# Loading q, k and v of a batch pair one step sooner in an attention + spectral-mix kernel

## The chip, the cores and the metric

The kernel runs on one core of a Trainium2 chip. The metric is device time in microseconds for one execution; lower is better. Seven runs of the kernel before the change are at hand, and one further execution that the hardware profiler recorded.

## The reference, cut to what matters

Batch 8, 8 heads, sequence 576, head width 64, so a model width of 512. All inputs and the output are float32.

```python
# attention with a forget gate
scores = q @ k.T / sqrt(64);  cum = cumsum(log(clip(f, 1e-4, 1)))
scores = where(causal, -1e9, scores + cum[:, None] - cum[None, :])
x = softmax(scores) @ v                     # -> (8, 576, 512)
# spectral mix
X = rfft(x, axis=1)[:, :64]                 # 64 modes
Yr = Xr @ w_r[m] - Xi @ w_i[m];  Yi = Xr @ w_i[m] + Xi @ w_r[m]   # per mode, 512 x 512
u = x + irfft(Y, n=576);  out = u + relu(u @ w_ch)
```

The weights w_r and w_i are 64 matrices of 512 x 512 each; they make up most of what is read from memory.

## The kernel before, in words

**Two stages.** In the first, attention runs as 32 steps (`NS`), numbered s. A step handles one head for two batches. Two steps with the same s // 2 form a *pair*, `pr`: it covers two batches and two heads, and there are 16 of them (`NPR`). They run over four channel blocks dc (two heads each), and in each block over four batch pairs bp. The loop over s stands at L649. In the second stage (from L683), the rest of the spectral mix, the product with w_ch and the output are made.

**What a pair needs.** `emit_loads(pr)` (L215) issues three DMAs, for k, q and v, from the Pool engine's queue into one of three staging sets (`STG` = 3, chosen by pr % 3). Only the first v goes by the SP queue. `emit_transposes(pr, what)` (L429) then copies the staged k, q or v on VectorE into a bf16 tile (kb, qb at L437; vb at L441), transposes it on TensorE (L455, tile tp), and copies the result out of PSUM: k and v on ScalarE (L468, L472), q on VectorE (L470). k and q of pair pr + 1 are handled at the even step of pair pr, v at its odd step (L658). A staging set is free for the next load once kb, qb and vb of its pair have been read from it.

**What a step does.** `emit_scores` (L499) makes scores in four pieces on TensorE (L507) and the exponential on ScalarE (L514). `emit_av` (L531) multiplies the exponentials of the step before by v (L552, tile pav) and divides by their sum on VectorE (L563, L574). `emit_vback` (L474) turns v back into rows (L479, then the copies L485 and L486). After the last step of a pair, `emit_dft` (L576) makes the 64 modes of the finished channels (L595; a first version for dc < 2 also has L620).

**The weights.** There are 64 weight tiles (`NT`), each of two DMAs of 512 KB, issued by `emit_w_load` (L91) on the Pool queue into a ring of nine buffers (`NRING`), named wb. `emit_modes(n)` (L118) consumes tile n: 32 small matmuls (L146) into the tile A, of which there is one PSUM buffer during attention, then one VectorE copy or addition out of it (L155, L157, or L161 for tiles 32 to 63). Only after that can the next tile's matmuls begin. From step 9 on, tiles 0 to 31 are consumed during attention, and each is followed by the load of the tile nine further on (L666 to L670). Tiles 32 to 63 need the spectrum of the last channel block and come after attention.

**What sets the order.** Every DMA of `pool_dma` (L88), and so every load of q, k, v and of weights after the first v, stays on the Pool queue in the order in which the program emits it. In steps 0 to 8 the loop mixes both kinds: `emit_loads(pr + 2)` at even steps (L651), weight tiles 2 to 8 by the rule of L653, and w_ch at step 9 (L655). The order of the instructions on TensorE, VectorE and ScalarE is not that of the source: a scheduler lays it down when the program is built, by when it reckons the operands of an instruction to be there. The copies kb, qb, vb of the first three pairs are the exception (L450).

## Time and profile before

| | us |
|---|---|
| median of 7 runs | 452.76 |
| lowest, highest | 450.14, 455.41 |
| the seven runs | 455.41, 450.17, 454.04, 450.58, 450.14, 453.12, 452.76 |
| the profiled execution, its own time | 454.45 |
| its span, first to last instruction | 452.6 |

The profile puts these shares of the span on the engines: PE (TensorE matmuls) 344.6 us or 76%, VectorE 239.9 us or 53%, ScalarE 197.6 us or 44%, Pool 138.9 us or 31%. The mean clock granted to TensorE was 0.774 of full speed. The core moved 97.27 MB by DMA, at 215 GB/s over the span.

In the profile, L146 is line 146 of the program; PE, PEld, DVE, ACT, POOL are TensorE's matmuls, its weight loads, VectorE, ScalarE and GpSimd. A timeline row gives the start in us, the duration, the engine, the line, the operation with output<-input, the number of instructions that were merged, and in square brackets the idle time ahead of it and what ended that idle time. A row of the window view gives a stretch of time, the busy us of each engine in it (with the number of instructions), the granted TensorE clock, the DMA share and GB/s. The three strips with 40 entries cut the span into slices of 11.3 us.

The pairs can be followed by the start of the copy kb, the first thing done with a pair's data:

| pair | 3 | 4 | 5 | 6 | 7 | 8 | 9 | 10 | 11 | 12 | 13 | 14 | 15 |
|---|---|---|---|---|---|---|---|---|---|---|---|---|---|
| kb starts, us | 45.53 | 58.74 | 70.34 | 87.66 | 107.67 | 127.11 | 147.28 | 165.75 | 184.14 | 201.76 | 218.71 | 236.53 | 255.91 |

### The profile page before, as it was taken

The numbers are of one execution on the slowest core, as the hardware profiler recorded it, in microseconds if no ns is written. First come the engines' busy times: TensorE is split into PE (matmuls) and PEld (weight loads), VectorE is DVE, ScalarE is ACT, GpSimd is POOL, SyncE is SP. The second block draws the span as 40 slices with busy tenths as digits, with TensorE's granted clock in tenths as the row PEclk, the third lists the DMA queues.
The fourth block names the chain that finished last, engine by engine and source line by source line (L and its number), as shares of the span: only waits on it lengthen the run. The fifth ranks groups of instructions, "written<-read, shape, count | busy, mean of one in ns | idle before, by whom it ended". The sixth has DMA issues, their size and how long they took to land.

```text
span 452.6 us, 11206 instructions
## 1 busy us (share of the span) xinstructions
PE 344.6 (76%) x4823; PEld 237.1 (52%) x4823; DVE 239.9 (53%) x614; ACT 197.6 (44%) x296; POOL 138.9 (31%) x195
## 2 busy tenths in 40 slices
PE   2786788987888879879778796999994247427992
PEld 1453656776666656656566574656673124323440
DVE  6677778675564655546547577333321002103993
ACT  3787478763536364364364554343330002102442
POOL 8233330532332232332332310123343232200660
PEclk9998799996756665566566778799995559856998
DMA  9999999899999999999999999699999999991697
GB/s 193 223 236 237 235 238 235 141 237 226 221 235 229 218 236 231 216 235 211 237 237 211 211 212 209 115 164 186 211 211 211 211 211 211 212 210 27 222 379 265
DMA packets 49920, 97.27 MB, mean 215 GB/s; under 512 B 3376, under 2 KB 12080, under 8 KB 49872
## 3 DMA queue, kind: packets, MB, share of 16 engines
q0 software_dynamic: 46240, 85.93, 97.4%
q1 hardware_dynamic: 3552, 10.50, 6.5%
q8 instruction: 38, 0.62, 0.5%
q10 hardware_dynamic: 80, 0.13, 0.1%
q14 instruction: 10, 0.08, 0.0%
HBM read 163.73 MB, written 9.44 MB: 383 GB/s over the span
## 4 chain that ended last, share of the span: by engine, by line
PE 46%; DMA 16%; ACT 12%; DVE 10%; issue 4%; POOL 0%; DVEq 0%; ACTq 0%
DMA wb<-in_moe_w_i_dram 16%; ACT E L514 8%; PE A L146 7%; PE pav L552 7%; PE pxw L731 7%; PE ps L507 7%; PE tp L455 5%; PE px L595 2%; DVE QTs L470 2%; PE vp L479 2%; PE ptr L720 2%; ACT KT L468 2%; ACT VT L472 2%; PE pz L834 1%; DVE E L529 1%
## 5 line engine op out<-in xcount | busy, mean ns | idle before, releaser
L514 ACT ACTIVATE E<-ps 128x1024 bf16<-128x1024 f32 (+1 forms) x128 | 101.1, 853 | 26.3 <-PE ps L507 17.7
L146 PE MATMUL A<-XT,wb 128*128 128x16 bf16 x2048 | 70.9, 182 | 45.1 <-DMA wb<-in_moe_w_i_dram 24.1
L146 PEld LDWEIGHTS <-wb 128*128 128x128 bf16 x2048 | 63.7, 101 | 56.7 <-DMA wb<-in_moe_w_i_dram 26.0
L89 POOL DMA_DIRECT2D wb<-in_moe_w_r_dram x65 | 43.2, 665 | 154.0 <-PE A L146 39.1
L507 PE MATMUL ps<-QTs,KT 64*128 64x64 bf16 (+4 forms) x384 | 59.0, 334 | 17.1 <-ACT E L514 15.7
L89 POOL DMA_DIRECT2D wb<-in_moe_w_i_dram x65 | 43.2, 665 | 65.1 <-DMA wb<-in_moe_w_r_dram 32.4
L552 PE MATMUL pav<-va,E 128*128 128x65 bf16 (+1 forms) x1088 | 57.1, 214 | 5.7 <-DVE x_all L574 4.0
L552 PEld LDWEIGHTS <-E 128*128 128x128 bf16 (+1 forms) x1088 | 47.4, 118 | 19.0 <-issue 8.1
L529 DVE TENSOR_TENSOR E<-E,trimask 128x256 bf16<-128x256 bf16 (+2 forms) x128 | 37.0, 301 | 22.4 <-ACT E L514 22.3
L161 DVE TENSOR_TENSOR YT<-A,Yacc 128x128 bf16<-128x128 f32 x24 | 8.9, 370 | 64.8 <-PE A L146 64.8
L472 ACT COPY VT<-tp 128x640 bf16<-128x640 bf16 (+1 forms) x32 | 23.3, 758 | 35.2 <-PE tp L455 35.1
L507 PEld LDWEIGHTS <-KT 64*128 64x128 bf16 x384 | 19.6, 101 | 33.0 <-issue 24.6
L731 PE MATMUL pxw<-wch,yy 128*128 128x512 bf16 x144 | 33.7, 384 | 0.0
L738 ACT CAST XW<-pxw 128x512 bf16<-128x512 f32 x36 | 20.3, 587 | 30.0 <-PE pxw L731 30.0
L468 ACT COPY KT<-tp 128x640 bf16<-128x640 bf16 (+1 forms) x32 | 22.0, 752 | 25.3 <-PE tp L455 25.3
L470 DVE COPY QTs<-tp 128x640 bf16<-128x640 bf16 (+1 forms) x32 | 23.2, 767 | 16.3 <-PE tp L455 16.3
L574 DVE TENSOR_TENSOR x_all<-pav,rcp 128x384 bf16<-128x384 f32 x64 | 29.0, 454 | 0.8
L563 DVE RECIPROCAL rcp<-pav 128x6 f32<-128x6 f32 x64 | 12.1, 190 | 27.6 <-PE pav L552 26.8
L879 POOL TENSOR_TENSOR uo<-uo 128x1024 f32<-128x1024 f32 x7 | 16.5, 2358 | 30.4 <-DVE uo L872 26.7
L750 ACT CAST yy<-pyw 128x512 bf16<-128x512 f32 x8 | 4.7, 586 | 48.2 <-PE pyw L743 48.2
L441 DVE TENSOR_TENSOR vb<-stv,wdec 128x1152 bf16<-128x1152 f32 x16 | 21.6, 1348 | 2.0 <-PE tp L455 2.0
L731 PEld LDWEIGHTS <-yy 128*128 128x128 bf16 x144 | 13.5, 99 | 16.8 <-DVE yy L725 4.5
(115 smaller groups left out, 467.9 us busy)
## 6 DMA issues: line engine op xcount, KB each, us to landing
wb<-in_moe_w_r_dram POOLq DMA_DIRECT2D x63, 512.0 KB, 16.2
wb<-in_moe_w_i_dram POOLq DMA_DIRECT2D x63, 512.0 KB, 16.5
stv<-in_v_dram POOLq DMA_DIRECT2D x15, 576.0 KB, 15.1
out_dram<-uo SPq DMA_DIRECT2D x16, 512.0 KB, 3.7
stk<-in_k_dram POOLq DMA_DIRECT2D x16, 288.0 KB, 15.4
stq<-in_q_dram POOLq DMA_DIRECT2D x16, 288.0 KB, 15.2
out_dram<-uo SPq DMA_DIRECT2D x7, 128.0 KB, 4.4
stv<-in_v_dram SPq DMA_DIRECT2D x1, 576.0 KB, 4.1
```

Of the source, the lines that this page charges most:

```text
L89: tc.keep_in_program_order(nc.gpsimd.dma_start(dst, src))
L146: nc.tensor.matmul(A[:, eb, mi, :], lhsT=w_of(mi, eb * 128), rhs=x_of(m), start=(i == 0), stop=(i == len(terms) - 1),)
L455: nc.tensor.transpose(tp[:, r - r0, :, :].rearrange("c h p -> c (h p)"), sb[:, r, :, :].rearrange("p b d -> p (b d)"), ident_bf[:, :],)
L468: nc.scalar.copy(rows(KTs[pr % 2][:, :, 0:S]), tv)
L470: nc.vector.tensor_copy(rows(QT[pr][:, :, :]), tv)
L472: nc.scalar.copy(rows(VTs[pr % 2][:, :, 0:S]), tv)
L507: nc.tensor.matmul(ps[:, b, o : o + n], lhsT=KTs[pr % 2][bs, h, jb * 128 : (jb + 1) * 128], rhs=QT[pr][bs, h, jb * 128 + c0 : jb * 128 + c ...
L514: nc.scalar.activation(E[:, :, piece * 512 : piece * 512 + w], ps[:, :, 0:w], ACT.Exp, scale=scale,)
L529: nc.vector.tensor_tensor(dg, dg, tr, ALU.mult)
L552: nc.tensor.matmul(pav[64 * half : 64 * half + w, slot, :], lhsT=E[:, b, c : c + (w - 1) * st + 1 : st], rhs=va[:, jb, b, :], start=(n == ...
L574: nc.vector.tensor_tensor(xo, pi, ri, ALU.mult)
L731: nc.tensor.matmul(pxw[:, :], lhsT=xT[:, eb, i * 128 : (i + 1) * 128], rhs=wch[:, eb, :], start=(eb == 0), stop=(eb == NDC - 1),)
```

## The change: the pair's loads move ahead of one weight tile

The call of `emit_loads` moves from the even step of a pair to the odd step before it. The pair that is loaded, the staging set and all shapes stay as they are.

```diff
         for s in range(NS + 1):
             pr, h = s // 2, s % 2
-            if h == 0 and pr + STG - 1 < NPR:
-                emit_loads(pr + STG - 1)
+            if s == 0:
+                emit_loads(STG - 1)
+            if h == 1 and pr + STG < NPR:
+                emit_loads(pr + STG)
             if s < 10 and nload < min(NRING, 3 + 3 * s // 4):
                 next_w()
             if s == 9:
```

At step s = 2 pr + 1 the program now loads pair pr + 3 into the set of pair pr, whose last copy (vb) is emitted at step 2 pr - 1. Before, the same load stood at step 2 pr + 2. The weight tiles and w_ch that lay between the two places on the Pool queue now come after the three DMAs.

## The prediction

> **What bounds the kernel.** I read the strips first, then Pool's timeline, then windows by pair, then PE's timeline. The strips (TensorE clock, DMA share, GB/s; slices of 11.3 us) suggest a kernel bound by its transfers:

> ```profile
> PEclk9998799996756665566566778799995559856998
> DMA  9999999899999999999999999699999999991697
> GB/s 193 223 236 237 235 238 235 141 237 226 221 235 229 218 236 231 216 235 211 237 237 211 211 212 209 115 164 186 211 211 211 211 211 211 212 210 27 222 379 265
> ```

> But the rate has two holes: 141 GB/s in the eighth slice, and 115 to 186 in the three slices from 283 us. Pool's timeline (start, duration, operation, idle time before it) has both:

> ```profile
> 66.23 0.74 POOL L89 DMA_DIRECT2D wch<-in_moe_w_ch_dram  x1 [1.85 <-DMA wb<-in_moe_w_i_dram]
> 83.16 0.62 POOL L89 DMA_DIRECT2D wb<-in_moe_w_r_dram  x1 [16.19 <-PE ps L507]
> ...
> 270.80 0.72 POOL L89 DMA_DIRECT2D wb<-in_moe_w_r_dram  x1 [8.75 <-PE A L146]
> 271.51 0.72 POOL L89 DMA_DIRECT2D wb<-in_moe_w_i_dram  x1
> 286.68 0.71 POOL L89 DMA_DIRECT2D wb<-in_moe_w_r_dram  x1 [14.45 <-PE A L146]
> ```

> At 66 us Pool has filled the ring of nine and stands until tile 0 is consumed (81.8 to 82.9 us). At 262 and 272 it stands again: the ring is full, the transfers are ahead of the arithmetic. The issue at 286.68 is tile 41, which needs the buffer of tile 32, and tile 32 needs the spectrum of the last pair. So **attention's arithmetic sets the time up to 286 us**, and what follows (166 us: 23 tiles at some 5.0 us each from 286.7, a thin start until 306, and about 42 us of output) hangs on that moment. The chain of waits agrees: its 16% of "DMA wb" all stand after 338 us.

> Is attention waiting for q, k, v? Pair 7's loads are issued at 84.4 to 85.8 us; such loads land about 15 us later (the issue table's median), so by 101; kb of pair 7 starts at 107.67. Pair 3: issued from 18.5, landed by 39, used at 45.53. Pair 5: 42.7 to 47.8, landed by 63, used at 70.34. No pair waits for its data. What is late is the *place* of the copy in VectorE's queue. PE's timeline and the windows before pair 7:

> ```profile
> 104.54 1.12 PE L146 MATMUL A<-XT,wb 128*128 128x16 bf16 x32 [0.52 <-DVE Yacc L155]
> 106.17 1.12 PE L146 MATMUL A<-XT,wb 128*128 128x16 bf16 x32 [0.52 <-DVE Yacc L155]
> 107.80 1.16 PE L146 MATMUL A<-XT,wb 128*128 128x16 bf16 x32 [0.52 <-DVE Yacc L155]
> ...
> 109.53 0.75 ACT L468 COPY KT<-tp 128x640 bf16<-128x640 bf16 x1 [5.56 <-PE tp L455]
> ```

> Weight tiles in a row, 1.63 us apart, each waiting 0.52 us for the single A buffer, ScalarE idle for 5.56 us, and pair 7 behind them. Windows (busy us of PE, PEld, DVE, ACT, POOL; clock; DMA; GB/s):

> ```profile
> 58.70:70.30 11.60, 9.87 (x142) 6.59 (x140) 10.07 (x30) 9.15 (x15) 3.42 (x5) 1.00 1.12 221
> 87.70:107.70 20.00, 16.95 (x366) 13.77 (x366) 13.21 (x41) 11.89 (x18) 6.54 (x11) 0.93 1.13 225
> 107.70:127.10 19.40, 16.16 (x239) 12.23 (x239) 11.29 (x32) 9.11 (x14) 6.04 (x10) 0.68 1.14 231
> ...
> 106.00:108.00 2.00, 1.32 (x39) 1.23 (x39) 0.79 (x3) 0.00 (x0) 0.62 (x1) 0.50 1.12 210
> ```

> Full clock until the row of tiles, then half clock for some 14 us; that pattern repeats for every later pair.

> **The change, part by part.** No instruction is added or dropped: the same 15 x 3 Pool loads. Two things move.

> *Pool's queue.* Pairs 3 and 5 keep their place (no weight tile lies between). Pairs 4, 6 and 8 to 15 pass one tile (two DMAs), pair 7 passes tile 9 and w_ch. Do the earlier loads wait for their staging set? Pair 7 would go at about 66 us; its set is last read by vb of pair 4, 61.6 to 62.9. Pair 6: about 52 us against 50.2. Pair 10: about 123 against 114.4. No new wait, though pair 6 has only some 2 us. Queued behind a late one would be weight tiles, which are used 25 us or more after issue here. w_ch slips by about 5 us to 71 and is used at 288. Cost: 0. The gain of pair 7 lying in the hole at 80 to 88 us is that of more bytes moved, which is lost again at 262 to 287, where the ring is full: 0.

> *The engines' order.* In the built program of the change, copies and transposes of a pair stand earlier among PE's work for pairs 4 to 7. Weight tiles consumed between one pair's k transposes and the next:

> ```
> pair to pair  5-6  6-7   7-8   8-9 9-10 10-11 11-12 12-13 13-14 14-15 15-end
> before         3    7     3     2   3    3     2     3     3     2     1
> after          1    4.7   5.3   3   3    2     3     3     2     3     2
> row of A matmuls that ends it:  before 116 (at 6-7); after 52 (at 7-8)
> ```

> So the first long row comes one pair later and is 64 matmuls shorter. (a) Two tiles fewer stand in that row: 2 x 1.63 = -3.3 us. (b) They return: one joins the row that ends 14-15, +1.6; the other (tile 31) now stands between the last vp and pav, where PE is idle 1.18 us anyway for the copy va (277.39 us, waiting on L485): 1.1 us of matmuls, 0. (c) Pair 7 now runs before the first row, at full clock. The same instructions at full and half clock, pair 6 against pair 7 (us): tk 0.68/1.12, tq 0.83/1.19, vp 0.44/0.69, px 0.89/1.40, scores 0.99/1.63, pav 0.78/1.23 and 0.69/1.02, px2 0.61/1.04, tv 0.44/0.74. Sum 6.35 against 10.06: -3.7 us, nearly all of it on the chain of waits, which between 108 and 118 us consists of PE. From below it is 0, if the clock drops within the pair all the same.

> [...] I take -2.3 for (c), nearer to the row; not all of it, because seven runs of one program spread over 5.3 us, so the slow stretches can't fall alike in each.

> Sum: -3.3 + 1.6 + 0 - 2.3 = **-4.0 us**. The tail keeps its 166 us: tile 40 is now issued some 9 us ahead of tile 32's end instead of 16, and needs about 7 (the quickest DMA of wb took 5.0 us to land, and there are two at some 2.2 us each). The profiled execution is 454.45, so 450.4; it lies 1.7 above the median. From the median of 452.76: **448.8 us**.

> **Rivals.**
> [...]
> 2. *The kernel is transfer-bound after all*, and the hole is what is gained: 4 us at 68 and 4 at 159 GB/s against 235 lack 2.8 + 1.3 = 4.1 us, giving 448.7 with the end of the weights 4.1 earlier. For it: DMA at 9 in nearly all slices. Against: the two ring waits at 262 and 272. Hence unlikely as a cause.
> 3. *Slower: the clock drops one pair earlier.* In pairs 4 and 5 all nine k transposes, then 16 pav matmuls, now stand ahead of the step's second score piece. If ScalarE runs dry there, PE waits for exponentials, thins out between 75 and 95 us, and pair 6 goes at half clock as well as pair 7: +3.7, with (a) and (b) -1.7, and up to 1.5 for the delayed pieces: 452.76 + 3.5 = 456.3. [...] Against: ScalarE copies KT until 62.0 before it takes that piece, so a delay of 1.2 us is mostly hidden.
> 4. *Nothing happens*, because no load was late: 452.8. The changed order of the engines speaks against it.

> **Numbers.** Half a per cent, 2.3 us, is what a measurement of this kernel can tell from no change. Forecast 0.46, rival 1 0.20, rival 2 0.04, rival 3 0.20, rival 4 0.10. The forecast's own range is 446.5 (all of (c), and 0.9 of run-to-run shift) to 450.5. The range takes in rivals 1, 2 and 4 and part of 3: 446 to 456. Faster by over 0.5% (under 450.5): forecast, rival 2 and a little of rival 1 = 0.52. Within: most of 1, rival 4, a little of 3 = 0.27. Slower: 0.21.

> **What would show it.** Right: the eighth slice's GB/s near 235, while kb of pair 8 starts 5 to 8 us sooner (119 to 122 us) and the clock stays at 1.00 until about 112; ScalarE's 5.56 us wait is gone or halved; tile 41 is issued near 283. [...] Rival 3: a low clock between 85 and 100. Wrong altogether: kb or vb waiting for stk, stq or stv, or Pool idle for a VectorE read ahead of one of these loads.

## The result and the profile after

The changed kernel takes 445.25 us (median of 12 runs, 443.68 to 449.87); the kernel before took 452.34 us in the 31 runs beside them. The ratio is **0.9872, with a 95% interval of 0.9842 to 0.9902**: of 452.34 that is 5.8 us less (4.4 to 7.1), where the prediction had 4.0 less. Some executions of a kernel fall in a slower state with a lower granted clock (of the 27 of the kernel before beside e1 to e4 it is 6, with a mean clock of 0.749 to 0.778, against 0.793 for the other 21); all ratios here leave them out, the medians do not, and so a quotient of two medians differs a little from the ratio. The profiled execution of the changed kernel took 446.41 us, its span is 444.0 us, and the mean granted clock 0.790. Its strips, in slices of 11.1 us:

```profile
PEclk9997699996557666668578698899995559756999
DMA  9999999999999999999999999899999999991697
GB/s 189 229 235 255 219 237 238 235 232 217 237 210 237 236 211 237 212 236 237 211 237 211 211 211 211 153 186 198 211 211 211 211 211 211 212 210 29 224 378 279
```

Of the two holes in the rate, the first is closed (eighth slice 235 in place of 141) and the second is still there (153 to 198). Pool's timeline shows both. The row at 70.87 is w_ch, which has slipped behind the loads of pair 7; the next ring wait ends at 82.37; the last row is tile 41.

```profile
70.87 0.76 POOL L89 DMA_DIRECT2D wch<-in_moe_w_ch_dram  x1 [0.40 <-DMA stv<-in_v_dram]
82.37 0.61 POOL L89 DMA_DIRECT2D wb<-in_moe_w_r_dram  x1 [10.74 <-PE vp L479]
...
263.61 0.72 POOL L89 DMA_DIRECT2D wb<-in_moe_w_r_dram  x1 [9.76 <-PE A L146]
270.19 0.71 POOL L89 DMA_DIRECT2D wb<-in_moe_w_r_dram  x1 [5.14 <-PE A L146]
279.06 0.71 POOL L89 DMA_DIRECT2D wb<-in_moe_w_r_dram  x1 [7.44 <-PE A L146]
```

Tile 41 is issued at 279.06, 7.6 us sooner than before (286.68), and the end of the span comes 8.6 sooner, 452.6 to 444.0. So nearly the whole gain is there when attention ends: from the end of tile 32 to the end of the span it is 166.2 us before and 165.2 after.

A single pair of profiles overstates the gain: 454.45 - 446.41 = 8.0 us, against 5.8 by the ratio. Over 21 executions of the kernel before, those that count in the ratios of e1 to e4 below, each 0.01 of mean granted clock goes with 1.16 us. The profiled one of before has 0.774, the profiled one of after 0.790, and 1.6 x 1.16 = 1.9 us is most of the 2.2 that are too much. Over many runs the two kernels have nearly the same mean clock (0.793 in those 21, 0.795 in the 12 of after), so the gain is not a higher clock on average.

Where was it made? The window view splits attention at 100 us. Columns: stretch, its length, busy us of PE, PEld, DVE, ACT and POOL with the number of instructions, granted clock, DMA share, GB/s. Before:

```profile
45.00:100.00 55.00, 47.67 (x762) 35.43 (x762) 42.40 (x122) 37.67 (x58) 17.27 (x26) 0.94 1.07 217
100.00:286.40 186.40, 152.40 (x2293) 114.46 (x2290) 110.48 (x298) 89.28 (x134) 51.73 (x77) 0.65 1.11 220
```

After:

```profile
45.00:100.00 55.00, 50.09 (x810) 37.62 (x811) 44.60 (x128) 38.99 (x60) 18.28 (x28) 0.93 1.14 231
100.00:278.80 178.80, 144.49 (x2240) 108.58 (x2240) 108.18 (x292) 88.59 (x134) 50.04 (x75) 0.69 1.13 222
```

The sums of matmuls are alike (3055 and 3050; some records of a trace are missing). In the first 55 us, nearly all at full clock in both, the changed kernel issues 48 more: PE is idle 4.9 us there and not 7.3. It enters the half-clock part with 48 matmuls less to do. At 186.4 / 2293 = 0.081 us each that is 3.9 us; the mix of matmuls isn't quite the same, so this is an estimate and not a sum. The largest part of what shrank is TensorE's waiting for ScalarE's exponentials (total us, times, longest; before, then after):

```profile
PE ps L507 <- ACT E L514: 2.4, 4, 0.8
PE ps L507 <- ACT E L514: 1.1, 4, 0.3
```

PE's timeline of the changed kernel around the k copy of pair 7 (98.87) shows how the work is mixed; the last row is ScalarE's, at pair 8:

```profile
98.53 0.61 PE L507 MATMUL ps<-QTs,KT 64*128 64x512 bf16 x6
99.07 0.44 PE L146 MATMUL A<-XT,wb 128*128 128x16 bf16 x9
99.38 0.68 PE L455 MATMUL tp<-ident_bf,kb 128*128 128x128 bf16 x9
100.43 0.50 PE L146 MATMUL A<-XT,wb 128*128 128x16 bf16 x11
...
102.50 0.78 PE L146 MATMUL A<-XT,wb 128*128 128x16 bf16 x23
...
104.30 0.69 PE L595 MATMUL px<-bas,x_all 128*128 128x128 bf16 x5
...
120.98 1.12 PE L146 MATMUL A<-XT,wb 128*128 128x16 bf16 x32 [0.52 <-DVE Yacc L155]
...
123.73 1.36 ACT L468 COPY KT<-tp 128x640 bf16<-128x640 bf16 x2 [3.28 <-PE tp L455]
```

A weight tile is cut into pieces of 9 to 23 matmuls that fill PE between the scores and the transposes. There is no row of tiles ahead of pair 7. The kernel before, in the same view, after its three tiles in a row:

```profile
108.79 1.12 PE L455 MATMUL tp<-ident_bf,kb 128*128 128x128 bf16 x9
...
112.56 0.69 PE L595 MATMUL px<-bas,x_all 128*128 128x128 bf16 x5
```

The px matmul of this step is the same piece of work in both: 104.30 against 112.56. By then 7 tiles have been consumed after and 10 before, while the matmuls of all other kinds are the same but for a few. Three tiles of the row are 3 x 1.63 = 4.9 us that the changed kernel still owes, so by this estimate 8.3 - 4.9 = 3.4 us is gained at equal work.

The clock, though, falls at the same moment in both profiled executions. The windows of the changed kernel:

```profile
80.70:98.90 18.20, 18.04 (x376) 14.23 (x375) 14.65 (x46) 13.69 (x21) 7.69 (x12) 1.00 1.15 232
98.90:122.50 23.60, 21.52 (x335) 15.27 (x329) 13.56 (x41) 12.44 (x18) 7.29 (x12) 0.61 1.12 230
...
102.00:104.00 2.00, 1.61 (x43) 1.50 (x41) 2.00 (x3) 1.29 (x3) 0.72 (x1) 0.98 1.13 212
104.00:106.00 2.00, 1.89 (x15) 1.09 (x13) 1.45 (x5) 0.22 (x1) 0.73 (x1) 0.50 1.12 213
```

It is at 0.50 from about 104 us, five microseconds after the k copy of pair 7 and with PE nearly full. Before, it fell at about 105. Most of pair 7 runs at half clock after all in this execution; it isn't so in every one (e1, in the part on the prediction).

One line of the page misleads. Its chain of waits now has 3% for "DMA stv", and the chain's order of time puts it here (start, length, what):

```profile
89.60 11.59 DMA stv<-in_v_dram
...
101.20 0.42 DVE Yacc L155
101.62 1.26 DVE vb L441
```

That looks like the copy vb of pair 7 waiting for its v. But v of pair 7 was issued at 69.74; the load issued at 89.60 is pair 8's. And VectorE's timeline has no idle time ahead of the two:

```profile
100.99 0.29 DVE L529 TENSOR_TENSOR E<-E,trimask 128x256 bf16<-128x256 bf16 x1 [0.62 <-ACT E L514]
101.20 0.42 DVE L155 COPY Yacc<-A 128x256 f32<-128x256 f32 x1
101.54 1.35 DVE L441 TENSOR_TENSOR vb<-stv,wdec 128x1152 bf16<-128x1152 f32 x1
```

With the queue of before, vb of this pair starts at 101.39 (order_only, below). So this copy did not wait for its load.

### The profile page after: what moved, and what is told of

It is laid out like the page before. It is cut to its first block, busy times and chain, and to the rows that moved or that the text cites. A ratio compares the mean times of both kernels' runs of the same rounds, so it can differ in the third digit from the quotient of the medians.

```text
span 444.0 us, 11207 instructions
## 1 busy us (share of the span) xinstructions
PE 338.9 (76%) x4823; PEld 233.2 (53%) x4823; DVE 240.0 (54%) x614; ACT 198.2 (45%) x296; POOL 138.5 (31%) x195
## 4 chain that ended last, share of the span: by engine, by line
PE 43%; DMA 19%; ACT 12%; DVE 9%; issue 4%; POOL 1%; DVEq 0%; ACTq 0%
DMA wb<-in_moe_w_i_dram 16%; ACT E L514 8%; PE pxw L733 7%; PE A L146 7%; PE pav L552 7%; PE ps L507 6%; PE tp L455 5%; DMA stv<-in_v_dram 3%; PE px L595 2%; DVE QTs L470 2%; PE ptr L722 2%; ACT KT L468 2%; PE vp L479 2%; PE pz L836 2%; DVE XT L609 1%
## 5 line engine op out<-in xcount | busy, mean ns | idle before, releaser
L146 PE MATMUL A<-XT,wb 128*128 128x16 bf16 x2048 | 70.9, 182 | 43.2 <-DMA wb<-in_moe_w_i_dram 23.9
L146 PEld LDWEIGHTS <-wb 128*128 128x128 bf16 x2048 | 63.9, 101 | 55.4 <-DMA wb<-in_moe_w_i_dram 25.8
L89 POOL DMA_DIRECT2D wb<-in_moe_w_r_dram x65 | 43.2, 665 | 151.6 <-PE A L146 47.6
L507 PE MATMUL ps<-QTs,KT 64*128 64x64 bf16 (+4 forms) x384 | 57.9, 326 | 17.6 <-ACT E L514 16.3
L89 POOL DMA_DIRECT2D wb<-in_moe_w_i_dram x65 | 43.1, 664 | 59.8 <-DMA wb<-in_moe_w_r_dram 28.1
L552 PE MATMUL pav<-va,E 128*128 128x65 bf16 (+1 forms) x1088 | 55.2, 210 | 4.1 <-DVE x_all L574 3.6
L552 PEld LDWEIGHTS <-E 128*128 128x128 bf16 (+1 forms) x1088 | 45.4, 114 | 19.9 <-issue 9.3
L507 PEld LDWEIGHTS <-KT 64*128 64x128 bf16 x384 | 19.3, 99 | 30.9 <-issue 22.1
L468 ACT COPY KT<-tp 128x640 bf16<-128x640 bf16 (+1 forms) x32 | 22.1, 755 | 21.9 <-PE tp L455 21.9
```

The costliest lines, as they stand in the source:

```text
L89: tc.keep_in_program_order(nc.gpsimd.dma_start(dst, src))
L146: nc.tensor.matmul(A[:, eb, mi, :], lhsT=w_of(mi, eb * 128), rhs=x_of(m), start=(i == 0), stop=(i == len(terms) - 1),)
L468: nc.scalar.copy(rows(KTs[pr % 2][:, :, 0:S]), tv)
L507: nc.tensor.matmul(ps[:, b, o : o + n], lhsT=KTs[pr % 2][bs, h, jb * 128 : (jb + 1) * 128], rhs=QT[pr][bs, h, jb * 128 + c0 : jb * 128 + c ...
L552: nc.tensor.matmul(pav[64 * half : 64 * half + w, slot, :], lhsT=E[:, b, c : c + (w - 1) * st + 1 : st], rhs=va[:, jb, b, :], start=(n == ...
```

## The experiments

The change does two things: it moves Pool's loads, and it makes the scheduler lay the other engines' instructions in another order. Most experiments take these apart. For that, the order of TensorE, VectorE and ScalarE was read out of one built kernel and laid down in another, as a list of runs that a small function turns into dependences between neighbours. They fix the order and nothing else (the class is NoSync); e8, in which the kernel before keeps its own order by this means, comes out at 1.0017. The comments in the edits below only say which order is laid down.

```diff
+def _pin_order(nc, tc):
+    traced = list(nc.cur_bb.bb.instructions)
+    for eng, runs in _ORDER.items():
...
+        for x, y in zip(seq, seq[1:]):
+            tc.add_manual_dep(y, x.name, mybir.DependencyInfo(
+                mybir.DependencyClass.NoSync, mybir.DependencyReason.DATA),
+                reason="issue order")
```

All were timed in three groups, each beside its own runs of the kernel before. Numbers of different groups are compared by their ratios:

| kernel | median, us | before, us | ratio | 95% interval |
|---|---|---|---|---|
| e1 order only | 446.53 | 451.88 | 0.9885 | 0.9843 to 0.9927 |
| e2 queue only | 450.78 | 451.88 | 0.9979 | 0.9955 to 1.0002 |
| e3 two steps sooner | 443.27 | 451.88 | 0.9821 | 0.9784 to 0.9859 |
| e4 interleaved throughout | 444.00 | 451.88 | 0.9833 | 0.9795 to 0.9870 |
| e5 early part | 447.86 | 451.46 | 0.9953 | 0.9930 to 0.9976 |
| e6 late part | 451.77 | 451.46 | 1.0026 | 0.9999 to 1.0053 |
| e7 from pair 6 | 450.57 | 451.46 | 0.9983 | 0.9942 to 1.0023 |
| e8 fewer bytes | 451.78 | 451.46 | 1.0017 | 0.9990 to 1.0043 |
| e9 short row only | 448.64 | 450.36 | 0.9963 | 0.9945 to 0.9982 |
| e10 pairs 4 and 5 only | 452.46 | 450.36 | 1.0054 | 1.0025 to 1.0082 |
| e11 fewer bytes, interleaved | 433.98 | 450.36 | 0.9638 | 0.9621 to 0.9656 |
| e12 order only again | 447.23 | 450.36 | 0.9937 | 0.9910 to 0.9964 |

### Order or queue: e1, e12, e2

Edit of e1 and e12: the kernel before, with its Pool queue, and

```diff
+        _pin_order(nc, tc)   # the order of the changed kernel
```

> The Pool queue of the kernel before, with TensorE, VectorE and ScalarE issuing in exactly the order that the changed kernel has. Theory A (the whole gain is the engines' order): ratio to before 0.987 (0.983 to 0.991), tile 32 done near 279 us, the hole in the transfers at 80 to 88 us back. Theory B (the gain is the earlier transfers): ratio 0.998 to 1.003, as before. A mixture lies between, and the second kernel then has the rest.

> The whole changed order with the Pool queue of before, a second time, as the fourth corner beside the early part alone and the short row alone on one chip. Both theories: 0.986 to 0.991.

Edit of e2: the changed kernel, with its Pool queue, and

```diff
+        _pin_order(nc, tc)   # the order of the kernel before
```

> The Pool queue of the changed kernel (loads ahead of a weight tile), with TensorE, VectorE and ScalarE issuing in exactly the order of the kernel before. Theory A: ratio to before 0.998 to 1.003, tile 32 done near 286 us, although the hole in the transfers at 80 to 88 us is filled. Theory B: ratio 0.987.

e1 and e12 are one and the same program. It gives 0.9885 in one group, as theory A said, and 0.9937 in another, above the 0.986 to 0.991 that was expected there (the intervals share 0.991 to 0.9927, some 3.3 to 4.1 us). In both groups it ran at a lower mean clock (0.785 and 0.786) than the runs of before (0.793 and 0.795); by the slope above that hides about 1 us. The queue alone gives 0.9979, an interval that ends just above 1. In e2 the first hole of the rate is closed as in the changed kernel (232 GB/s in the eighth slice), and that is worth about 1 us, between nothing and 2. **Most of the gain is the order of the engines.** The theory that the earlier transfers are the gain falls for this change; a small share of theirs can't be told from none.

### Do bytes count before: e8

```diff
     def emit_w_load(n):
+        if n in (20, 24):
+            wtiles[n] = wtiles[n - 1]
+            return
         dc, g = tile_of(n)
```

The order of the engines is pinned to that of before.

> Kernel before with its own order of the engines, but tiles 20 and 24 are not loaded; their matmuls read the buffers of tiles 19 and 23. About 10 us less of transfers (two tiles at some 5.0 us). Theory arithmetic (transfers are ahead before 286 us): no change, ratio 0.998 to 1.000. Theory transfers (rival 2): up to -10 us, a ratio down to 0.978.

Some 10 us of transfers less, and the time stays: 1.0017 (0.9990 to 1.0043). Before 286 us the kernel before is not bound by its transfers, as was read from the two ring waits.

### Which part of the order: e5, e6, e9

These three are mixtures of the two orders on the queue of before. e5 takes the changed order up to the k copies of pair 8 and the old one behind; e6 is the reverse; e9 is the old order but for two weight tiles, which leave the row before pair 7.

```diff
-        _pin_order(nc, tc)   # the order of the changed kernel
+        _pin_order(nc, tc)   # e5: changed up to pair 8, then as before; e6: the reverse
+                             # e9: as before, row of 52 in place of 116 before pair 7
```

> Pool queue of the kernel before. TensorE, VectorE and ScalarE follow the changed order up to the k copies of pair 8 - but the two weight tiles that the change takes out of the long row are put back into it, so that the row of 116 matmuls stands whole, only now between pairs 7 and 8 - and the order of before from there on. Three theories. P, the interleaving of pairs 4 to 7 is what pays: nearly the whole gain of the order, a ratio near 0.989 (some 447 us). Q, the tiles taken out of the row and worked off later are what pays: 1.000. The prediction's sum: only its term (c) is left, -2.3 of 452, so 0.995.

> The complement: order of before up to the k copies of pair 8 (pairs 4 to 6 as before, the row of 116 before pair 7), then the changed order, which leaves one tile fewer before each following pair and works the last one off between vp and pav at the end. P: 1.000. Q: a ratio near 0.989. The prediction's sum: (a) and (b) only, -1.7 of 452, so 0.996.

> Pool queue and order of the kernel before in every pair, but two weight tiles (64 matmuls and their two copies) are taken out of the row of 116 before pair 7 and worked off where the changed order has them: one more between pairs 8 and 9, and the last one between vp and pav of the last pair. This is the prediction's (a) + (b) alone. By its sum: -1.7 of 452, ratio 0.996. Theory S, the two parts add up (the whole order over the early part alone, 0.9885 / 0.9953): 0.993, some 449. Theory T, the shorter row is worth something only together with the earlier pairs 4 to 7: 0.999 to 1.002.

e5 gives 0.9953, 2.1 us less (1.1 to 3.2): the prediction's sum, not theory P. e9 gives 0.9963, 1.7 us less (0.8 to 2.5): the prediction's sum again, and theories S (0.993) and T fall: the shorter row pays in the old surroundings too, by this much and no more. PE's timeline of e9 shows the row that is left:

```profile
104.05 0.76 PE L146 MATMUL A<-XT,wb 128*128 128x16 bf16 x20
105.33 1.12 PE L146 MATMUL A<-XT,wb 128*128 128x16 bf16 x32 [0.52 <-DVE Yacc L155]
106.28 1.12 PE L455 MATMUL tp<-ident_bf,kb 128*128 128x128 bf16 x9
```

One whole tile and one wait of 0.52, where the kernel before has three. e6 keeps the long row and pushes one tile from between pairs 8 and 9 to the end: 1.0026, no gain, where 0.996 was expected by the prediction's sum. The sum counts the tiles of the long row, and e6 leaves that row whole. Here a tile taken from a short row of 64 paid nothing; two taken from the long row paid.

The two parts multiply to 0.9953 x 0.9963 = 0.9916, inside both intervals of the whole order (0.9843 to 0.9927 and 0.9910 to 0.9964). So they add up within what can be told, and no third part is needed.

What does the early part consist of, if the clock falls at the same time? The first window of e5, where the row of 116 stands whole, only later:

```profile
45.00:100.00 55.00, 49.20 (x792) 36.61 (x792) 44.24 (x127) 37.98 (x59) 17.23 (x26) 0.94 1.06 216
```

and that of e12, the whole order:

```profile
45.00:100.00 55.00, 50.80 (x827) 38.09 (x828) 44.45 (x129) 40.16 (x61) 17.90 (x27) 0.94 1.11 225
```

Up to 100 us e5 issues 30 matmuls more than the kernel before, e12 65 more. In these profiles the early part shows as a denser PE during the full-clock stretch, and not as a longer stretch. That is a reading of single executions and no proof: e10 (below) issues 15 more there and gains nothing.

### Which pairs: e7, e10

e7 takes the old order up to the k copies of pair 6 and the changed one behind; e10 is the reverse.

```diff
-        _pin_order(nc, tc)   # the order of the changed kernel
+        _pin_order(nc, tc)   # e7: before up to pair 6, then changed; e10: the reverse
```

> Order of before up to the k copies of pair 6, the changed order from there: pairs 4 and 5 as before, but pair 7 runs ahead of the (short) row of 52. If the gain sits in pair 7 passing the row, or in the two tiles, the ratio is that of the whole order, 0.989. If it sits in pairs 4 and 5 (interleaved copies in the early, full-clock part, where kb of pair 6 came 7 us sooner), it is near 0.995 or above.

> Changed order up to the k copies of pair 6, order of before from there; the row of 116 stays before pair 7. Only pairs 4 and 5 differ. If the early part's gain (0.9953) comes from pairs 4 and 5: 0.995 to 0.996. If it comes from pair 7 passing the long row (the prediction's (c)): 0.999 to 1.001.

For e10 neither expectation holds; e7 came where it was expected if the gain sat in pairs 4 and 5, which e10 then excludes. Pairs 4 and 5 alone make the kernel *slower*, 1.0054; from pair 6 on alone, with the short row and pair 7 ahead of it, gives 0.9983, no change that can be told; e7's interval still has room for the 0.9963 of the short row. Yet e5, which is e10 with pairs 6 and 7 moved as well, is at 0.9953, so that on top of pairs 4 and 5 the move of the next two is worth about 1%. e7 and e10 together change every pair, and their product, 1.0037, is far from the 0.9916 of the whole order. So the early part doesn't divide by pairs. e10 ran at a lower mean clock than its runs of before (0.784 to 0.795), which by the slope above is about 1.2 us of its 2.4; why that mixture draws a lower clock was not tried and stays open.

### How far it goes: e3, e4, e11

e3 moves the loads of a pair one step further:

```diff
-            if h == 1 and pr + STG < NPR:
+            if h == 0 and pr + STG < NPR:
                 emit_loads(pr + STG)
```

e4 has the queue of the changed kernel and an order in which the copies of every pair are interleaved, so that no row of tiles stands ahead of any. The scheduler laid it down for a build with small weight DMAs, and it was read out of that build.

```diff
+        _pin_order(nc, tc)   # an order without rows of tiles
```

> The loads one step sooner still than in the changed kernel (pair p + 3 at the even step of pair p). The order that is built then interleaves one more pair's copies with the exponentials (pair 8), and its first long row of weight tiles stands before pair 9. Theory A: one more pair without a long row ahead of it, another 2 to 4 us, ratio to before 0.978 to 0.984. Theory B: nothing more than the changed kernel, 0.987, or worse where a load has to wait for its staging set.

> The Pool queue of the changed kernel, and an order of TensorE, VectorE and ScalarE in which the copies and transposes of every pair, not only of pairs up to 7, stand among the exponentials of the pair before, with no long row of weight tiles. Theory A: pairs 8 to 15 take 16 instead of 18 us each, so another 10 to 16 us off, ratio to before 0.95 to 0.965, the granted clock near 1.0 to 250 us. If the clock falls at about 104 us whatever the order is: only the ScalarE idle time goes, ratio 0.97 to 0.985. Theory B: as the changed kernel, 0.987.

e3 comes where theory A had it, at 0.9821. e4 does not: theory A had 0.95 to 0.965, and it comes at 0.9833. Both lie a little below the changed kernel's 0.9872, though the intervals overlap. But e4 finishes tile 32 at 263.5 us, 9 us ahead of e3 (272.45), and ends no sooner. GB/s of e3:

```profile
GB/s 190 229 263 237 237 238 224 221 237 210 237 237 211 236 217 230 237 216 232 229 220 211 211 211 211 211 209 211 211 211 211 211 211 211 211 173 22 229 382 274
```

The hole after 283 us is gone. In e4 it is gone as well, and its chain of waits by engine (share of the span) is another one:

```profile
DMA 60%; PE 23%; ACT 5%; DVE 5%; issue 3%; SPq 1%; POOL 1%; DVEq 0%; ACTq 0%; POOLq 0%
```

Transfers hold 60% of the chain, where they held 16% before. e11 is e4 with tiles 20 and 24 left out as in e8.

> The kernel in which the copies of every pair are interleaved (0.9833), with tiles 20 and 24 not loaded; their matmuls read the buffers of tiles 19 and 23. Theory: there attention ends early enough (tile 32 at 263.5) that the transfers set the end, so some 4 us of the 10 are gained until tile 41 waits for tile 32 again: about 440 us, ratio 0.973 to 0.976. If the transfers do not bind there either: 0.983, as with all tiles.

It takes 433.98 us, 10.0 less than e4 by the times and 8.8 by the ratios: nearly all of the two tiles' transfer time, more than the 4 us that were expected, and the same edit gave the kernel before nothing. **The bound has changed sides**: in the kernel before it is attention's arithmetic, in the one without rows of tiles it is the bytes. Bytes were not left out of the changed kernel itself; it still has its hole (153 to 198 GB/s) and a ring wait of 7.44 us, so where it stands is read and not shown.

## Why the prediction was right

*What bounds the kernel.* Right: "attention's arithmetic sets the time up to 286 us". e8 shows that the transfers don't, and the tail of 166 us is kept (165.2 after).

*Pool's queue at 0.* Right within what can be told (e2). The hole at 80 to 88 us closed as foreseen and bought about 1 us, at most 2. No load waited for its staging set: Pool's idle time ahead of pair 7's k load is 2.42 us, but that set's last reader, vb of pair 4, started at 60.17, seven microseconds earlier.

*(a) and (b), -1.7.* Right, -1.7 measured (e9, 0.8 to 2.5). ScalarE's wait of 5.56 us at the end of the long row is 3.28 after, neither gone nor halved.

*(c), -2.3.* The size is right (e5: -2.1, 1.1 to 3.2, for the whole early part); the cause came about in some executions only. The -2.3 itself was the author's choice between 0 and the listed 3.7, and no run shows that share alone. In the profiled one of the changed kernel, "Pair 7 now runs before the first row, at full clock" failed: the clock is at 0.50 from 104 us, and the mark "the clock stays at 1.00 until about 112" was missed. Ahead of the drop are only the k and q transposes (0.68 and 0.82 us, against 1.12 and 1.19): 0.8 us of the listed 3.7. But e1 and e12, one program, differ in just this. Pair 7 in e1, then in e12:

```profile
98.72:118.97 20.25, 18.06 (x335) 13.94 (x329) 13.36 (x40) 12.22 (x18) 5.95 (x10) 0.87 1.13 225
97.67:121.28 23.61, 21.63 (x335) 15.36 (x329) 13.53 (x40) 12.45 (x18) 6.80 (x12) 0.60 1.13 223
```

The same 335 matmuls take 3.4 us less where the clock stays up, near the listed 3.7. So the prediction did well to take only a part of (c), on the ground that slow stretches don't fall alike in each execution; how often pair 7 has the full clock, one profile of each run can't say. The rest of the early gain is what the prediction did not list: PE's idle time before 100 us shrank from 7.3 to 4.9 us.

On the clock, rival 3 reckoned that a PE that thins out lowers it. Measured by busy time that fails: PE is busy 1.42 and 1.61 of 2 us just ahead of the drop, then 1.89 and 2.00 at half clock, while the kernel before keeps a clock of 1.00 from 62 to 64 us with PE busy 1.03 of 2 us. Measured by the columns that the matmuls stream it fits the traces of the kernel before and of the changed one (last section): the stretches with the row of tiles (1536 and 1088 columns), and the one ahead of the drop in the changed kernel (2512), are the thin ones. No long gap stands ahead of that drop: the longest in the rows from 96.8 us up to it is 0.45 us.

*The rivals.* A gain of (a) and (b) alone, which gives 452.76 - 1.7 = 451.1, did not come about, although in two of the three profiles with the changed order the clock drops inside pair 7 and stays low (a mean of 0.61 and 0.60 over the pair, against 0.87 in e1): the early part gave its 2.1 us besides (e5). Rival 2 (transfers) is wrong for this change and right for the next one (e11). Rival 3 didn't happen: the clock is 1.00 from 80.7 to 98.9 us. Yet its first half, pairs 4 and 5 moved and nothing gained behind them, is slower by 0.5% when it is done alone (e10), though not by rival 3's mechanism: in e10's profile the nine k transposes at 71.12 and 88.17 us take 0.66 and 0.68 us, as pair 6's do at full clock, and not 1.12. Rival 4 is excluded by the interval.

*The marks.* Eighth slice near 235: 235. k copy of pair 8 at 119 to 122: 122.47, and 118.97 and 121.28 in e1 and e12. Tile 41 near 283: 279.06, off by the clock of the two profiled executions and by what the change gave beyond 4.0.

What was underestimated is the whole, 5.8 against 4.0, and the interval begins at 4.4. By the ratio the 452.76 of the prediction become 447.0, inside its range; the plain median of 445.25 lies just under the 446 at which that range begins. Order (0.9885 and 0.9937) and queue (0.9979) leave room for either to be the larger part of the missing 1.8; the runs don't settle it.

## What to carry to other kernels

Moving a load can change the time through the scheduler alone: pin the order of one build on the queue of the other before crediting the DMA. Look for the longest row of one kind of work that stands ahead of a chain's next link: here shortening that row paid, and shortening a short one didn't. Don't read the clock of a stage from one profile: two executions of one program differed by 3.4 us in one pair. And before tuning the arithmetic further, leave out a few bytes: the kernel before shrugged at 10 us of transfers, the one without rows of tiles gave nearly all of them back.

## What the runs showed of the hardware

The row of tiles before pair 7 in the kernel before fills the pieces from 101.5 and 104.9 us with 1536 and 1088. The last full-clock piece of the changed kernel, from 100.5 us, has 14 matmuls of 128 columns, 41 of a tile and two score matmuls of 32: 2512, after 4028 in the piece before. At half clock PE is nearly full (1.89 and 2.00 of 2 us from 104 us) and still streams only 2637 and 2923 in the next two. Between 2500 and 3400 the count alone doesn't tell: in the kernel before, 3021 columns are followed by half clock at 169.8 us and by full clock at 241.4. This is what the two traces have in common; no run was made to test it.

The half-clock stretches of the kernel before that begin between 104 and 280 us last 13.7 us in six cases, 10.2 in two and 30.7 in one (from 163 us), so the pattern of pair 7 does not return alike at every later pair.

*What it is worth.* The mean granted clock differs between executions of one program and explains a part of the spread: 1.16 us for each 0.01 over the 21 executions of the kernel before, 0.88 and 1.13 in the two other groups. In e3 and e4, which are at or near the bound of the bytes, the slope is gone (+0.14 and -0.15 us over six executions each), and the spread is small: e3's six lie between 442.96 and 444.1, e4's between 442.84 and 445.82. The weights stream at 211 GB/s in nearly every slice once nothing holds them up, while slices with q, k and v among them reach 237.
